# Bucket bits by four 32-column products into one bank, and one reading engine for each count bank, in a hash-masked attention and MoE kernel

## The chip, the cores and the metric

The kernel runs on one core of a Trainium2 chip. The metric is device time in microseconds, from the start of the program to its end; runs are compared by their median.

A core has a matrix engine (TensorE, PE in the rows), whose weight loads (PEld) overlap its products, and three engines for elementwise work: VectorE (DVE), ScalarE (ACT) and GpSimd (POOL). Each takes its own instructions in order. Transfers are issued on a fifth queue, SyncE's (SP). Products land in PSUM, in banks of 128 partitions x 512 floats.

## The reference

Attention with a bucket mask, then a gated MLP (SiLU), then an MLP (ELU). The part that the change touches is the mask: a query sees only keys of its own bucket, and a bucket is the six signs of the head's vector times `proj`.

```python
q_bits = (np.einsum('bhsd,dk->bhsk', q, proj) > 0).astype(np.int64)
k_bits = (np.einsum('bhsd,dk->bhsk', k, proj) > 0).astype(np.int64)
q_bucket = np.sum(q_bits * powers, axis=-1)
k_bucket = np.sum(k_bits * powers, axis=-1)
mask = q_bucket[:, :, :, None] == k_bucket[:, :, None, :]
scores = scale * np.matmul(q, k.transpose(0, 1, 3, 2))
scores = np.where(mask, scores, -1000000000.0)
scores = scores - np.max(scores, axis=-1, keepdims=True)
attn = np.exp(scores)
attn = attn / (np.sum(attn, axis=-1, keepdims=True) + 1e-09)
return np.matmul(attn, v).astype(np.float32)
# then, on x of (1536, 512), with x = norm(attention):
#   y   = (silu(xn @ w_gate) * (xn @ w_val)) @ w_out      d_ff 1536
#   out = elu(y @ w_in) @ w_out2                          d_ff 2048
```

There are 2 batches of 8 heads, 768 positions and 64 channels a head, all in fp32; the MLP weights arrive as 64-bit floats.

## The kernel before

**Pairs.** The 16 heads are taken in eight pairs (index `j`; the head in the pair is `a`). A pair's inputs come in six transfers of 384 KB: for each head `qk` (query over key, 64 channels each, 128 partitions), `kk` (key twice) and `qq` (query twice).

**Operands.** A head's scores are one product over 256 rows in two steps of 128 partitions, in the fast fp32r format. The operands are `tq` (query side) and `tk` (key side), each of two planes of 128 x 768. Three quarters of them hold the rounded vector and its rounding rest; the last 64 rows of plane 1 hold the bucket code: `tk` a +-1 per bucket, `tq` a value of 2^60 in the row of its own bucket, so that a score outside the bucket falls far below the others. GpSimd makes the query side in `operand_q`: `upper` casts the upper 64 partitions (L405), `lower` multiplies the lower 64 by the scale (L412), a transfer copies the result (`dup`, L416) and `lo` subtracts (L420). ScalarE and GpSimd make the key side in `operand_k` (L375, L382).

**Bits and counts.** `prep_bits` multiplies a pair's `qk` by `proj` in plain fp32, for each half of the positions (`hf`, 384 columns) once: two products, one a head, summed into one bank `ps_b` (L442). The columns of `pj` are laid so that the query and key bits of both heads stand in 24 partitions. VectorE compares that bank with zero into `bitt` (L447, 24 x 384, two a pair); a row of ones in `bitt` carries a constant. `prep_count` then multiplies `bitt` by a table `wsel` for the query side (`i` = 0) and the key side (`i` = 1) and each half: four banks `ps_c` a pair (L461), 64 partitions of a bank to each head. Each bank is read twice (`hot`), once a head, into `tq` or `tk`: by VectorE (L472) and by ScalarE (L470), as `HOT = ('DVE', 'ACT', 'ACT', 'DVE')` says, so that each bank has one reader on either engine.

**The rest of attention.** Per 128 queries: four score products into a double bank `ps_s` (L517), a maximum (VectorE `nm`, L524), an exponential (ScalarE `p`, L534); per 256 queries three groups of transposes into a bank `ps_p` (L562), split into rounded part and rest `pt` (ScalarE L570, VectorE L574; or GpSimd L583, L586), and products with the values in `ps_v` (L609). There are four single banks, shared by `ps_b`, `ps_c`, `ps_p`, `ps_v` and the norm's banks, and two double banks. While pairs run, the engines also turn the first MLP weights into two fp32r tensors each (L851 to L900).

**The MLPs** follow on TensorE as three-pass fp32r products (`ps_h` L949, `ps_y` L1034, `ps_o` L1089), with the other engines splitting the hidden values and preparing further weights beside them.

**The order.** Every step is a task in a list with its engine, a planned cost and what it needs. The numbers in `ORDER` are the tasks in the order in which they are issued, over all engines; that order is fixed in the file, and the planned costs do not act at run time. Each engine runs its own instructions in that order and waits for what they need. At the start TensorE runs products without use (`ps_w`, L1150) until inputs are there.

Of the kernel before, what the change touches and what calls it, by code (L numbers as in the profile page):

```python
# [225 lines left out]
def kernel(  # L226
# [53 lines left out]
    def f(ap):  # L280
        return ap.bitcast(F32)

    ident = const.tile([128, 128], F32, name="ident")
    pj = const.tile([128, 2, 128], F32, name="pj")
    wsel = const.tile([128, 2, 128], F32R, name="wsel")
    bitt = [const.tile([128, S], F32R, name=f"bitt{i}") for i in range(2)]
    ones = const.tile([128, 128], F32, name="ones")
# [986 lines left out]
```

## Time and profile before

| | us |
|---|---|
| median of 3 runs (838.7 to 840.76) | 839.86 |
| the profiled execution | 840.58 |
| its span in the trace | 838.8 |
| TensorE busy, of the span | 816.9 (97%) |
| VectorE busy | 602.1 (72%) |
| ScalarE busy | 416.8 (50%) |
| GpSimd busy | 328.1 (39%) |

The profiled execution took 1.78 us more than its span and 0.72 us more than the median. The shares of the whole span mix two stages: the pairs, up to about 265 us, and the MLPs behind them. A matmul's busy time is modelled, and a product is counted for longer than the distance to the next one. So the distance between products, read from the chain of waits, says what a product costs, and the stretches say which engine has slack.

### The profile page before, as it was taken

Reading aid. Unit: us, or ns where it says so; the run is one execution under the profiler, and the core shown is the slowest. Engines: PE = TensorE matmul, PEld = TensorE weight load, DVE = VectorE, ACT = ScalarE, POOL = GpSimd, SP = SyncE. Lnnn points to the kernel's source line nnn. Section 1 sums busy time; section 2 is a strip of 40 time slices with the busy share of each in tenths; the row PEclk is TensorE's granted clock in tenths of the full one; section 3 lists DMA queues with packets and bytes.
Section 4 is the critical chain, followed back from the end, with each engine's and each line's share of the span. In section 5 each row is a group of like instructions: output and inputs, shape, how many; then the busy total and the mean of one; then the engine's idle time right before and its main releaser. Section 6 shows DMA issues by size and latency. Waiting matters only on the chain.

```text
span 838.8 us, 11843 instructions
## 1 busy us (share of the span) xinstructions
PE 816.9 (97%) x4498; PEld 714.1 (85%) x4498; DVE 602.1 (72%) x933; ACT 416.8 (50%) x785; POOL 328.1 (39%) x273
## 2 busy tenths in 40 slices
PE   7999999999899999999999999999999999999998
PEld 6898888888789999898888888888788888888887
DVE  4788899999998683543555564879666768677676
ACT  3898998977888553431222321335454242332321
POOL 7899987898988501100111212021012011110210
PEclk8999999999999999999999999999999999999999
DMA  6525842252103002200302123130322300021004
GB/s 214 165 68 169 275 143 83 67 159 69 39 1 114 1 1 93 71 26 1 131 21 76 51 61 115 39 103 13 111 76 87 102 24 26 26 76 50 1 1 150
DMA packets 28473, 64.99 MB, mean 77 GB/s; under 512 B 2816, under 2 KB 3584, under 8 KB 28416
## 3 DMA queue, kind: packets, MB, share of 16 engines
q1 hardware_dynamic: 28416, 64.24, 23.8%
q8 instruction: 35, 0.57, 0.3%
q14 instruction: 22, 0.18, 0.1%
HBM read 57.94 MB, written 3.15 MB: 73 GB/s over the span
## 4 chain that ended last, share of the span: by engine, by line
PE 77%; DVE 11%; ACT 7%; issue 2%; POOL 1%; DMA 1%; SPq 0%; ACTq 0%; DVEq 0%; POOLq 0%
PE ps_h L949 36%; PE ps_o L1089 15%; PE ps_y L1034 10%; PE ps_v L609 5%; PE ps_s L517 5%; PE ps_p L562 4%; DVE pt L574 2%; DVE nm L524 2%; ACT p L534 2%; ACT pt L570 2%; PE ps_b L442 1%; DVE wf L867 1%; DMA kk<-in_heads_dram 1%; DVE wf L874 1%; DVE ya L1046 1%
## 5 line engine op out<-in xcount | busy, mean ns | idle before, releaser
L900 POOL TENSOR_TENSOR wlo<-wf,whi 128x768 fp32r<-128x768 f32 (+1 forms) x54 | 88.4, 1650 | 448.3 <-ACT whi L896 387.4
L949 PE MATMUL ps_h<-xn,whi 128*128 128x512 f32 (+2 forms) x768 | 190.2, 336 | 0.0
L949 PEld LDWEIGHTS ps_h<-xn,whi 128*128 128x128 f32 x768 | 133.8, 189 | 11.9
L995 ACT CAST h<-hf 128x512 fp32r<-128x512 f32 (+1 forms) x87 | 52.1, 606 | 179.3 <-DVE hf L980 60.5
L949 PE MATMUL ps_h<-xn,wlo 128*128 128x512 f32 (+2 forms) x384 | 128.9, 336 | 0.0
L1089 PE MATMUL ps_o<-whi,h 128*128 128x512 f32 (+1 forms) x388 | 118.6, 387 | 0.4 <-DVE ya L1046 0.4
L949 PE MATMUL ps_h<-y,whi 128*128 128x512 f32 x384 | 118.2, 389 | 0.0
L517 PE MATMUL ps_s<-tk,tq 128*128 128x384 f32 x384 | 90.8, 359 | 8.7 <-ACT p L534 6.4
L609 PE MATMUL ps_v<-pt,vv 128*128 128x256 f32 x576 | 94.4, 294 | 2.1 <-DVE pt L574 1.0
L524 DVE TENSOR_REDUCE nm<-ps_s 128x1 f32<-128x768 f32 x96 | 90.8, 947 | 7.4 <-PE ps_s L517 6.5
L999 DVE TENSOR_TENSOR h<-hf,h 128x512 fp32r<-128x512 f32 (+1 forms) x87 | 64.5, 756 | 41.5 <-ACT h L995 41.3
L1034 PE MATMUL ps_y<-h,whi 128*128 128x512 f32 (+1 forms) x312 | 91.6, 374 | 0.8 <-DVE ya L1046 0.7
L534 ACT ACTIVATE p<-ps_s,nm 128x768 f32<-128x768 f32 x96 | 87.1, 908 | 8.5 <-DVE nm L524 7.7
L574 DVE TENSOR_TENSOR pt<-ps_p,pt 128x512 fp32r<-128x512 f32 x120 | 80.0, 682 | 12.9 <-ACT pt L570 12.0
L562 PE MATMUL ps_p<-ident,p 128*128 128x128 f32 x576 | 84.6, 278 | 2.9 <-DVE pt L574 2.2
L1089 PEld LDWEIGHTS ps_o<-whi,h 128*128 128x128 f32 x388 | 72.6, 188 | 15.5 <-DVE ya L1046 0.8
L974 ACT ACTIVATE sg<-ps_h 128x512 f32<-128x512 f32 (+1 forms) x87 | 49.4, 580 | 72.3 <-PE ps_h L949 53.3
L949 PEld LDWEIGHTS ps_h<-y,whi 128*128 128x128 f32 x384 | 72.1, 188 | 14.9
L609 PEld LDWEIGHTS ps_v<-pt,vv 128*128 128x128 f32 x576 | 78.8, 189 | 5.4 <-DVE pt L574 2.2
L562 PEld LDWEIGHTS ps_p<-ident,p 128*128 128x128 f32 x576 | 67.6, 142 | 12.0 <-DVE pt L574 5.1
L949 PEld LDWEIGHTS ps_h<-xn,wlo 128*128 128x128 f32 x384 | 72.6, 189 | 5.7
L517 PEld LDWEIGHTS ps_s<-tk,tq 128*128 128x128 f32 x384 | 64.3, 191 | 14.9 <-ACT p L534 10.8
(91 smaller groups left out, 1366.4 us busy)
## 6 DMA issues: line engine op xcount, KB each, us to landing
wraw<-in_moe_w_out_dram SPq DMA_DIRECT2D x12, 768.0 KB, 4.7
qq<-in_heads_dram SPq DMA_DIRECT2D x16, 384.0 KB, 4.2
qk<-in_heads_dram SPq DMA_DIRECT2D x16, 384.0 KB, 4.7
kk<-in_heads_dram SPq DMA_DIRECT2D x16, 384.0 KB, 4.0
wraw<-in_moe_w_in_dram SPq DMA_DIRECT2D x8, 768.0 KB, 5.6
wraw<-in_moe_w_out_dram SPq DMA_DIRECT2D x10, 512.0 KB, 3.6
vn<-in_v_dram SPq DMA_DIRECT2D x8, 384.0 KB, 3.5
wraw<-in_moe_w_gate_dram SPq DMA_DIRECT2D x4, 768.0 KB, 5.4
```

The lines of the kernel that those rows point to most:

```text
L517: nc.tensor.matmul(st[B_][:, hf, 0:HS], lhsT=tq[:, x, c * 128:(c + 1) * 128], rhs=tk[:, x, hf * HS:(hf + 1) * HS], start=(x == 0), stop=(x ...
L524: nc.vector.tensor_reduce(out=st["nm", u, cc], in_=st[B_][:, :, 0:HS], axis=AX.XY, op=ALU.max, negate=True,)
L534: nc.scalar.activation(out=halves(st["p", u][:, cc]), in_=st.pop(B_)[:, :, 0:HS], func=AF.Exp, bias=st["nm", u, cc], scale=1.0, accum_out= ...
L562: nc.tensor.transpose(out=st[B_][:, o:o + 128], in_=p[:, cc, (2 * n + kt) * 128:(2 * n + kt + 1) * 128], identity=ident,)
L574: nc.vector.tensor_tensor(out=pt[:, 1], in0=st.pop(B_), in1=f(pt[:, 0]), op=ALU.subtract)
L609: nc.tensor.matmul(st[B_][:, 0:256], lhsT=st["vv", j][:, a, 2 * n + kt, :], rhs=pt[:, x, kt * 256:(kt + 1) * 256], start=(n == seq[0] and ...
L900: nc.gpsimd.tensor_tensor(out=l, in0=s["w"], in1=f(h), op=ALU.subtract)
L949: nc.tensor.matmul(ps[:, o:o + ln], lhsT=w[wp][:, kk, ft * 128:(ft + 1) * 128], rhs=t[xp][:, s:s + ln], start=(kk == 0 and n == 0), stop=( ...
L995: nc.scalar.copy(out=st["h", g, blk, ft][:, 0, 0:bw], in_=s["hf"])
L999: nc.vector.tensor_tensor(out=h[:, 1, 0:bw], in0=s["hf"], in1=f(h[:, 0, 0:bw]), op=ALU.subtract)
L1034: nc.tensor.matmul(s["ps"][:, 0:bw], lhsT=wo[wp][:, ft, m * 128:(m + 1) * 128], rhs=h[:, xp, 0:bw], start=(ft == 0 and i == 0), stop=(ft = ...
L1089: nc.tensor.matmul(s["ps"], lhsT=h[:, xp, t * 128:(t + 1) * 128], rhs=wo[wp][:, ft, ds], start=(ft == 0 and i == 0), stop=(ft == n - 1 and ...
```

## The change

It does five things.

1. **Bits.** `pj` becomes 128 x 32: the six columns of `proj` for the query channels, six for the key channels, the rest zero. A pair's four products (two halves, two heads) each go to their own group of 32 partitions of one bank. `bitt` becomes 128 x 384. One comparison a pair, with a threshold per partition (`floor`: 0, and -1 in the first row of each group, which makes the row of ones).
2. **Counts.** `wsel` has a half more as an index, with zeros in the rows of the other half; the four count products a pair stay, each over all of `bitt`.
3. **Readers.** `HOT = ('DVE', 'ACT')`: VectorE reads both heads of a query bank, ScalarE both heads of a key bank. The number of reads is the same on either engine.
4. **Query operand.** `upper` and `lower` become one GpSimd instruction over all 128 partitions with a scale per partition and a second multiplication by 1.0.
5. **Order and planned costs.** A new `ORDER` for the whole program, and some planned costs.

```diff
+BITS = 1.8
-HOT = ('DVE', 'ACT', 'ACT', 'DVE')
+HOT = ('DVE', 'ACT')
-QENG = ["Pool"] * 16
 ORDER = [
-    9, 0, 6, 5, 1, 7, 56, 50, 53, 2, 8, 48, 51, 57, 59, 49, 28, 10, 12, 13, 14, 15, 16, 17, 54, 55, 11, 60, 61, 68,
...
-    pj = const.tile([128, 2, 128], F32, name="pj")
-    wsel = const.tile([128, 2, 128], F32R, name="wsel")
-    bitt = [const.tile([128, S], F32R, name=f"bitt{i}") for i in range(2)]
+    pj = const.tile([128, 32], F32, name="pj")
+    wsel = const.tile([128, 2, 2, 128], F32R, name="wsel")
+    bitt = [const.tile([128, S // 2], F32R, name=f"bitt{i}") for i in range(2)]
+    floor = const.tile([128, 1], F32, name="floor")
...
         def both():
-            nc.scalar.activation(
-                out=operand(j, a, 0)[:, 0, cs], in_=st["x", j, a, 2][:, cs], func=AF.Copy, scale=share[:, 1:2]
-            )
+            nc.gpsimd.tensor_scalar(
+                out=operand(j, a, 0)[:, 0, cs], in0=st["x", j, a, 2][:, cs], scalar1=share[:, 1:2], scalar2=1.0,
+                op0=ALU.mult, op1=ALU.mult,
+            )
...
-            plan.add("Pool", 0.12 + n * 0.00092, upper, [X_], los, prio)
...
-                plan.add("Pool", 0.12 + n * 0.00092, lower, [X_], his, prio)
+        plan.add("Pool", 0.17 + n * 0.00105, both, [X_, "share"], his + los, prio)
...
         def pe():
             st[B_] = bank("ps_b")
-            for a in range(2):
-                nc.tensor.matmul(
-                    st[B_][:, 0:HS], lhsT=pj[:, a], rhs=st["x", j, a, 0][:, cs], start=(a == 0), stop=(a == 1)
-                )
+            for hf in range(2):
+                for a in range(2):
+                    g = 64 * hf + 32 * a
+                    nc.tensor.matmul(
+                        st[B_][g:g + 32, 0:HS], lhsT=pj, rhs=st["x", j, a, 0][:, hf * HS:(hf + 1) * HS],
+                        start=True, stop=True,
+                    )
 
         def bits():
             nc.vector.tensor_scalar(
-                out=bitt[j % 2][0:M, cs], in0=st.pop(B_)[0:M, 0:HS], scalar1=0.0, scalar2=None,
-                op0=ALU.is_gt,
-            )
+                out=bitt[j % 2], in0=st.pop(B_)[:, 0:HS], scalar1=floor[:, 0:1], scalar2=None, op0=ALU.is_gt,
+            )
...
-                st[B_][:, 0:HS], lhsT=wsel[:, i, :], rhs=bitt[j % 2][:, cs], start=True, stop=True
+                st[B_][:, 0:HS], lhsT=wsel[:, hf, i, :], rhs=bitt[j % 2], start=True, stop=True
...
-            eng = HOT[2 * i + a]
+            eng = HOT[i]
...
-    dma(lambda: nc.sync.dma_start(out=pj, in_=proj), 128 * 1024, [], ["pj"], -29.93)
+    dma(lambda: nc.sync.dma_start(out=pj, in_=proj), 128 * 128, [], ["pj"], -29.93)
```

The transfers at the start stand in another order on SyncE's queue. Before (names as above; `wtmp` is the table, `vn` the values):

```order
L322 DMA qq<-in_heads_dram 128x768
L322 DMA qk<-in_heads_dram 128x768
L1144 DMA pj<-in_proj_dram 128x256
L322 DMA qk<-in_heads_dram 128x768
L322 DMA kk<-in_heads_dram 128x768
L1137 DMA wtmp<-in_table_dram 128x256
L322 DMA kk<-in_heads_dram 128x768
L322 DMA qq<-in_heads_dram 128x768
```

And now:

```order
L321 DMA qk<-in_heads_dram 128x768
L1126 DMA pj<-in_proj_dram 128x32
L321 DMA qk<-in_heads_dram 128x768
L321 DMA qq<-in_heads_dram 128x768
L321 DMA kk<-in_heads_dram 128x768
L1119 DMA wtmp<-in_table_dram 128x256
L332 DMA vn<-in_v_dram 128x768
L405 DMA tq<-tq 64x384
L321 DMA kk<-in_heads_dram 128x768
L321 DMA qq<-in_heads_dram 128x768
```

The second `qk` moved from fourth to third place, behind a smaller `pj`; the first `kk` stayed fifth, and the second moved back from seventh to ninth.

On ScalarE at the start of the program, the reads of pair 0's count banks (L470, now L452) stand about the key operands (L375, now L374). Each `kk` serves one head; the buffer numbers tell the banks apart. Before:

```order
L375 ACTIVATE tk_110<-kk_108,share_86 128x384 x2
L375 ACTIVATE tk_131<-kk_118,share_86 128x384
L470 ACTIVATE tk_110<-ps_c_163 64x384
L470 ACTIVATE tk_110<-ps_c_168 64x384
L470 ACTIVATE tq_134<-ps_c_171 64x384
L470 ACTIVATE tq_134<-ps_c_160 64x384
```

And now:

```order
L374 ACTIVATE tk_137<-kk_135,share_87 128x384 x2
L452 ACTIVATE tk_137<-ps_c_149 64x384
L452 ACTIVATE tk_137<-ps_c_155 64x384
L452 ACTIVATE tk_167<-ps_c_149 64x384
L374 ACTIVATE tk_167<-kk_164,share_87 128x384
```

The first head's reads no longer stand behind the second head's `kk`, and ScalarE no longer reads query banks.

On VectorE in pair 1's preparation, the reads of count banks among the other work. Before:

```order
L472 TENSOR_SCALAR tq_251<-ps_c_299 64x384
L472 TENSOR_SCALAR tk_318<-ps_c_311 64x384
L574 TENSOR_TENSOR pt_325<-ps_p_320,pt_325 128x512
L524 TENSOR_REDUCE nm_345<-ps_s_333 128x1
L627 TENSOR_TENSOR ot_342<-ps_v_267,ot_342 64x256
L524 TENSOR_REDUCE nm_375<-ps_s_358 128x1
L447 TENSOR_SCALAR bitt1_83<-ps_b_352 24x384
```

And now:

```order
L454 TENSOR_SCALAR tq_261<-ps_c_306 64x384
L454 TENSOR_SCALAR tq_309<-ps_c_306 64x384
L555 TENSOR_TENSOR pt_319<-ps_p_314,pt_319 128x512
L505 TENSOR_REDUCE nm_345<-ps_s_328 128x1
L454 TENSOR_SCALAR tq_309<-ps_c_349 64x384
L505 TENSOR_REDUCE nm_358<-ps_s_353 128x1
L454 TENSOR_SCALAR tq_261<-ps_c_349 64x384
```

Both reads of a bank now stand on VectorE: next to each other for bank 306, with a maximum between them for bank 349. A comparison of pair 1 that stood among these rows is gone.

## Rows read from the trace of the kernel before

**Rows 1.** Stretches: busy us (instructions) of each engine, TensorE clock, DMA share, GB/s
```profile
0.00:14.07 14.07, 9.58 (x47) 7.56 (x47) 4.95 (x12) 4.63 (x8) 10.04 (x18) 1.00 0.83 278
14.07:264.50 250.43, 237.27 (x1604) 213.25 (x1605) 226.58 (x342) 212.46 (x432) 224.07 (x193) 0.99 0.34 106
290.00:838.80 548.80, 544.59 (x2683) 468.32 (x2681) 355.09 (x557) 184.30 (x316) 77.38 (x48) 1.00 0.18 59
```

**Rows 2.** The page's chain that ended last: shares of the span
```profile
PE 77%; DVE 11%; ACT 7%; issue 2%; POOL 1%; DMA 1%; SPq 0%; ACTq 0%; DVEq 0%; POOLq 0%
PE ps_h L949 36%; PE ps_o L1089 15%; PE ps_y L1034 10%; PE ps_v L609 5%; PE ps_s L517 5%; PE ps_p L562 4%; DVE pt L574 2%; DVE nm L524 2%; ACT p L534 2%; ACT pt L570 2%; PE ps_b L442 1%; DVE wf L867 1%; DMA kk<-in_heads_dram 1%; DVE wf L874 1%; DVE ya L1046 1%
```

**Rows 3.** Pieces of that chain, up to 275 us: start, us, what
```profile
22.04 1.29 PE ps_b L442 x4
...
132.83 2.13 POOL tq L412
```

**Rows 4.** Instructions on ps_b: ns min/median/max, first and last start us
```profile
L442 PE MATMUL ps_b<-qk,pj x64: 483/486/590, 6.6 to 208.7; 128*128 128x384 f32 x64
L447 DVE TENSOR_SCALAR bitt<-ps_b x16: 534/537/546, 9.1 to 210.8; 24x384 fp32r<-24x384 f32 x16
```

**Rows 5.** Reads of ps_c, the same columns
```profile
L470 ACT ACTIVATE tq<-ps_c x16: 475/488/492, 12.5 to 220.6; 64x384 fp32r<-64x384 f32 x16
L472 DVE TENSOR_SCALAR tq<-ps_c x16: 538/540/551, 13.4 to 215.9; 64x384 fp32r<-64x384 f32 x16
```

**Rows 6.** Who waited for whom: us in total, times, longest us
```profile
PEld ps_s L517 <- ACT p L534: 10.8, 16, 1.7
...
ACT tq L470 <- DVE tq L472: 5.9, 6, 1.3
...
PEld ps_p L562 <- DVE pt L574: 5.1, 10, 0.9
...
DVE tq L472 <- ACT tq L470: 4.1, 4, 2.5
ACT tk L470 <- DVE tk L472: 3.7, 4, 1.5
...
DVE tk L472 <- ACT tk L470: 2.8, 3, 1.7
```

**Rows 7.** GpSimd's groups by form: busy us, mean ns
```profile
L412 POOL TENSOR_SCALAR tq<-qq 64x768 fp32r<-64x768 f32 x14 | 29.9, 2133 | 1.2
...
L405 POOL CAST tq<-qq 64x768 fp32r<-64x768 f32 x14 | 11.9, 848 | 0.4
...
L741 POOL TENSOR_SCALAR z<-z 128x384 f32<-128x384 f32 x2 | 1.0, 514 | 0.2
```

**Rows 8.** Timeline of the start: start us, us, what [idle before, releaser]
```profile
8.16 2.20 PE L442 MATMUL ps_b<-qk,pj 128*128 128x384 f32 x6 [0.77 <-DMA qk<-in_heads_dram]
...
9.18 1.12 ACT L375 ACTIVATE tk<-kk,share 128x384 fp32r<-128x384 f32 x2 [7.19 <-DMA kk<-in_heads_dram]
...
9.59 0.34 DVE L1155 CAST wsel<-wtmp 128x256 fp32r<-128x256 f32 x1
...
9.87 2.94 POOL L382 TENSOR_TENSOR tk<-kk,tk 64x384 fp32r<-64x384 f32 x3
...
11.13 0.61 ACT L375 ACTIVATE tk<-kk,share 128x384 fp32r<-128x384 f32 x1 [0.83 <-DMA kk<-in_heads_dram]
...
13.42 0.55 DVE L472 TENSOR_SCALAR tq<-ps_c 64x384 fp32r<-64x384 f32 x1 [2.47 <-ACT tq L470]
...
14.07 1.55 PE L517 MATMUL ps_s<-tk,tq 128*128 128x384 f32 x6 [2.10 <-DVE tq L472]
```

**Rows 9.** Stretches of the start, columns as in rows 1
```profile
17.00:19.00 2.00, 2.00 (x7) 2.00 (x8) 1.22 (x3) 1.14 (x3) 1.85 (x3) 0.50 0.49 172
...
23.00:25.00 2.00, 2.00 (x16) 1.87 (x15) 1.83 (x4) 1.54 (x5) 1.94 (x3) 1.00 0.04 10
```

**Rows 10.** TensorE's waits from 268 us on, columns as in rows 6
```profile
PE ps_y L1034 <- DVE ya L1046: 0.7, 2, 0.5
```

More of the change, by code (lines that the diff above doesn't have):

```diff
@@ L398, in both @@
         def both():
-            nc.scalar.activation(
-                out=operand(j, a, 0)[:, 0, cs], in_=st["x", j, a, 2][:, cs], func=AF.Copy, scale=share[:, 1:2]
-            )
-        def upper():
-            out, in_ = operand(j, a, 0)[up, 0, cs], st["x", j, a, 2][up, cs]
-            nc.gpsimd.tensor_copy(out=out, in_=in_)
-        def lower():
-            out, in_ = operand(j, a, 0)[dn, 0, cs], st["x", j, a, 2][dn, cs]
-            if how == "mixed":
-                nc.scalar.activation(out=out, in_=in_, func=AF.Copy, scale=QSCALE)
-            else:
-                nc.gpsimd.tensor_scalar(out=out, in0=in_, scalar1=QSCALE, scalar2=None, op0=ALU.mult)
+            nc.gpsimd.tensor_scalar(
+                out=operand(j, a, 0)[:, 0, cs], in0=st["x", j, a, 2][:, cs], scalar1=share[:, 1:2], scalar2=1.0,
+                op0=ALU.mult, op1=ALU.mult,
+            )
         def dup():
@@ L422, in operand_q, with prep_bits @@
         his, los, dups = ([okey(j, a, 0, (p, h)) for h in cols] for p in ("hi", "lo", "dup"))
-        if how == "ACT":
-            plan.add("ACT", act(n) + 0.15, both, [X_, "share"], his + los, prio)
-        else:
-            plan.add("Pool", 0.12 + n * 0.00092, upper, [X_], los, prio)
-            if how == "mixed":
-                plan.add("ACT", act(n) + 0.05, lower, [X_], his, prio)
-            else:
-                plan.add("Pool", 0.12 + n * 0.00092, lower, [X_], his, prio)
+        plan.add("Pool", 0.17 + n * 0.00105, both, [X_, "share"], his + los, prio)
         dma(dup, 64 * n * 4, his, dups, prio)
         plan.add("Pool", pool(n), lo, [X_], los, prio)
-    def prep_bits(j, hf, prio):
-        cs = slice(hf * HS, (hf + 1) * HS)
-        B_ = ("bank", "b", j, hf)
-        M = 4 * NB
+    def prep_bits(j, prio):
+        B_ = ("bank", "b", j)
         def pe():
             st[B_] = bank("ps_b")
-            for a in range(2):
-                nc.tensor.matmul(
-                    st[B_][:, 0:HS], lhsT=pj[:, a], rhs=st["x", j, a, 0][:, cs], start=(a == 0), stop=(a == 1)
-                )
+            for hf in range(2):
[5 more added lines that the diff above has]
+                    )
         def bits():
             nc.vector.tensor_scalar(
-                out=bitt[j % 2][0:M, cs], in0=st.pop(B_)[0:M, 0:HS], scalar1=0.0, scalar2=None,
-                op0=ALU.is_gt,
-            )
-        plan.add("PE", 8 * mm(HS) - 0.09, pe, [*(("h3", "x", j, a, 0) for a in range(2)), "pj"], [B_], prio)
-        plan.add("DVE", dve(HS), bits, [B_, "bitt"], [(("bits", j), hf)], prio)
+                out=bitt[j % 2], in0=st.pop(B_)[:, 0:HS], scalar1=floor[:, 0:1], scalar2=None, op0=ALU.is_gt,
+            )
+        plan.add("PE", BITS, pe, [*(("h3", "x", j, a, 0) for a in range(2)), "pj"], [B_], prio)
+        plan.add("DVE", dve(HS), bits, [B_, "floor"], [("bits", j)], prio)
     def prep_count(j, i, hf, prio):
@@ L486, in prep @@
         p = prio
-        for hf in range(2):
-            prep_bits(j, hf, p)
-            p += step
+        prep_bits(j, p)
+        p += 2 * step
         for i in range(2):
@@ L1122, in setup_bits @@
     def setup_bits():
-        for t in bitt:
-            nc.vector.memset(f(t), 0.0)
-            nc.vector.memset(f(t[32:33]), 1.0)
+        nc.vector.memset(floor, 0.0)
+        for g in range(4):
+            nc.vector.memset(floor[32 * g:32 * g + 1], -1.0)
+        nc.vector.memset(f(wsel), 0.0)
     def setup2():
@@ L1152, with spread_table @@
     for n in range(WARM):
-        plan.add("PE", 0.218, lambda n=n: warm(n), ["ident"], [("bank", "warm")], 1e6)
+        plan.add("PE", 0.25, lambda n=n: warm(n), ["ident"], [("bank", "warm")], 1e6)
     dma(ld_table, 128 * 1024, [], [("h3", "wtmp")], -29.92)
-    plan.add("DVE", 0.35, lambda: nc.vector.tensor_copy(out=wsel, in_=st["wtmp"]), [("h3", "wtmp")], ["wsel"], -28)
+    def spread_table():
+        for hf in range(2):
+            rows = slice(64 * hf, 64 * hf + 64)
+            nc.vector.tensor_copy(out=wsel[rows, hf], in_=st["wtmp"][rows])
+    plan.add("DVE", 0.55, spread_table, [("h3", "wtmp"), "wzero"], ["wsel"], -28)
     load_v(0, -27)
@@ L1236, in _laid_out @@
     v = v.reshape(B * H // 2, 2, S // 128, 128, D).transpose(0, 3, 1, 2, 4)
-    wide = np.zeros((2, D, 2, 128), proj.dtype)
-    table = np.zeros((128, 2, 128), np.float32)
+    wide = np.zeros((2, D, 32), proj.dtype)
+    table = np.zeros((4, 32, 2, 128), np.float32)
     for i in range(2):
-        for a in range(2):
-            o = (2 * i + a) * nb
-            wide[i, :, a, o:o + nb] = proj
+        o = 1 + i * nb
+        wide[i, :, o:o + nb] = proj
+        for g in range(4):
+            a = g % 2
             for n in range(2 ** nb):
                 for b in range(nb):
-                    table[o + b, i, 64 * a + n] = 1.0 if n >> b & 1 else -1.0
-                table[32, i, 64 * a + n] = 1.0 - bin(n).count("1") - i
-    return dict(rest, heads=heads, v=v, proj=wide.reshape(2 * D, 2, 128), table=table)
+                    table[g, o + b, i, 64 * a + n] = 1.0 if n >> b & 1 else -1.0
+                table[g, 0, i, 64 * a + n] = 1.0 - bin(n).count("1") - i
+    return dict(rest, heads=heads, v=v, proj=wide.reshape(2 * D, 32), table=table.reshape(128, 2, 128))
 def kernel(**inputs):
```

24 lines of the change are left out of this document (12 added, 12 removed), and 277 rows, old and new, of the table ORDER.

## Prediction

> **What bounds the kernel now.** I read the chain that ended last first, over the whole span [rows 2]: 77% of it is TensorE, and the three MLP products alone are 61%. Then I cut the span where the stages change [rows 1]. From 290 us to the end TensorE is busy 544.6 of 548.8 us; the longest wait there after 268 us is 0.7 us in total [rows 10], and the rest of the idle time is the last addition and store. The work of that stage is the same before and after, so it moves with the moment at which the pairs are done and gives nothing itself.
>
> The pairs are another matter. From 14.07 us to 264.50, where the first MLP product starts (250.4 us), TensorE is busy 237.3, VectorE 226.6, GpSimd 224.1, ScalarE 212.5 [rows 1]. No engine is full, all four are at 85 to 95%, and they wait for each other in turn: the largest waits of TensorE there are on the exponential (10.8 us) and on the subtraction that frees a bank (5.1 us) [rows 6]. So a microsecond taken from one engine is worth between nothing and a microsecond, and I look for work that leaves both of the fullest engines. Before 14.07 us TensorE does nothing for the scores: that is the start, whose length is a chain of loads and small steps [rows 8].
>
> **1. The products for the bits.** There are 32 products in the program before and after. The trace has 64 records of them [rows 4], two a product. On the chain two products take 1.29 us [rows 3], so a record's distance to the next is 1.29/4 = 0.32 us, and a pair costs 2.58 us. No trace of before shows products in groups of 32 partitions. The bounds: all four side by side, two records long, 0.64 us; none side by side, 2.58 us, and the switch to narrow groups and back lets the pipeline empty each time. For emptying I take what a record lasts beyond its distance, 0.486 - 0.32 = 0.16 us [rows 4], twice: 2.91 us. Between them I reason from the order of the instructions. TensorE takes them in turn; the two records of one product write the same group and must follow each other; the second of one and the first of the next are in different groups. So five distances, 1.61 us, and one tail of 0.16: 1.8 us. I take that, since it needs only what the records show. It saves 0.8 us a pair, 5.6 us in the seven pairs behind the start; the ends are +2.3 and -13.6 us.
>
> The Trainium skill has a rule for more and one for less. Its page TensorEngine Tiling (Array Packing), section Theoretical Speedup, gives up to four times for an output of 32 columns; the page TensorE: Matmul & The Clock Gate, Part 3, gives 2.38 times measured with three column tiles. By 2.38 (an estimate from that page) a pair would cost 1.1 us and the seven would save 10.5 us. The first page's Key Properties say that a change of tiling mode drains the engine, which speaks against the change. No row here shows either.
>
> **2. The comparisons.** Sixteen of 0.537 us become eight of the same length, since the columns stay 384 and only the partitions grow [rows 4]. Seven of the saved ones lie behind the start: VectorE does 3.8 us less. A dearer one, by the threshold read per partition, would show in a longer row; I take the old duration.
>
> **3. One reader a bank.** The number of reads and their durations (0.54 on VectorE, 0.49 on ScalarE [rows 5]) stay. What goes is the turn: the second reader waits for the first. VectorE waited 4.1 + 2.8 us for ScalarE's reads and ScalarE 5.9 + 3.7 us for VectorE's [rows 6]. Of VectorE's 6.9 us, 2.5 belong to the start [rows 8]; 4.4 remain. What takes their place is a read behind other work of the same engine, which costs the engine nothing but holds the bank (rival below). So VectorE's part of the stretch shrinks by 3.8 + 4.4 = 8.2 us if the rest of its work keeps its pace. ScalarE gets 9.6 us more slack, which I count at nothing: it has 38 us of it [rows 1].
>
> **4. The query operand on GpSimd.** A cast of 0.848 and a multiplication of 2.133 us become one instruction on 128 partitions [rows 7]. The nearest row for the new one is the multiplication with two operations on 128 x 384, 0.514 us, twice that for 768 columns: 1.03 us. The far ends are 0.85 and 2.13. GpSimd loses 14 x (2.98 - 1.03) = 27 us, at least 12. It was late for others in one place that I find on the chain, where the old multiplication stands with 2.13 us [rows 3]. So I take 0, with 3 us for the lower end. The transfer of the result and the subtraction behind it also start earlier, which helps the same step.
>
> **5. The start.** Scores run without a break from 14.07 us, when VectorE's first `tq` is done; that read began at 13.42 after 2.47 us of waiting for ScalarE's read of the same bank [rows 8]. ScalarE was late because it stood at the second `kk`, whose wait ended at 11.13. In the new order that key step stands behind the first head's two key reads, and no query read waits for ScalarE. New times, from the rows: the second `qk` comes one load earlier (1.95 us for 512 KB between the two `kk`, 9.18 to 11.13, so 1.46 a load, and 0.43 for the smaller `pj`): 8.16 - 1.9 = 6.3. Bits until 8, comparison until 8.7. The table's cast is at 9.59 as before at the latest, since its load is sixth again. Counts at 9.9, VectorE's read until 10.8. ScalarE's two key operands end at 10.3 as now, its two key reads at 11.4. GpSimd's two key rests start when the first key operand is there (one of two in 1.12 us, so 9.75) and take 0.98 us each (three in 2.94): 11.7. So the scores start at about 12.2 instead of 14.07: -1.8 us; the ends are 0 (the table or a load late) and -2.2.
>
> The clock hangs on the start. The granted clock is 0.50 (1.2 GHz) from 17 to 21 us while TensorE is busy without a break, and 1.00 (2.4 GHz) from 23 on [rows 9]; before the fall it had waited 2.1 us for a read [rows 8]. A start with fewer waits may be spared that: some 5 us of work at half speed, so at most -2.5. A start with another gap may have it for 2 us longer. I take 0.
>
> **6. The new order as such** changes what waits where in all of the 250 us. But for the edits above it holds the same instructions, and the first MLP product stands behind the same 1601 products of TensorE. I count it at 0 and give it 4 us either way.
>
> **The sum.** Behind the start TensorE alone would give -5.6 and VectorE alone -8.2. The two depend on each other, so I take the middle, -7. With the start, -8.8. The profiled execution took 840.58 us, so 831.8; the median of the runs lies 0.7 lower, so **831.1 us**. With the order's 4 us and the ends of the start (1.8 and -0.4) this case reaches from 826.5 to 837.
>
> **Rivals.**
>
> *All four products side by side.* Then a pair costs 0.64 + 0.16 = 0.8 us and TensorE saves 12.4 us behind the start, and VectorE follows, because its waits on scores shrink. 840.6 - 1.8 - 12.4 = 826.4, on the runs' scale 825.7; with the clock spared 823. For it: the groups share no partition. Against: two records of one product stand in one group, and VectorE at 226.6 - 3.8 of some 238 us would be at 94%. Chance 0.13. It is what the Trainium skill's page TensorEngine Tiling (Array Packing), section Theoretical Speedup, promises for 32 columns.
>
> *The bits do not get shorter.* The groups run one after the other and both switches cost a tail: 2.91 us a pair, +2.3 us behind the start. TensorE then sets the pace, and VectorE's 8.2 us become waiting: 840.6 - 1.8 + 2.3 = 841.1, on the runs' scale 840.4. That is the change not doing what it says. For it: nothing in the trace shows two products at once. Chance 0.07. The Trainium skill's rule that a change of mode drains the engine (the same page, Key Properties) would work towards it.
>
> *The gain goes to steps that are not touched.* VectorE has more room, but the maximum, the exponential and the two halves of `pt` are on the chain with 2% of the span each [rows 2], and they are as long as before. Then only the start and a share of the bits come through: 840.6 - 1.8 - 1 = 837.8, or 837.1 on the runs' scale, up to 839.5 if the start gives half. Chance 0.11.
>
> *Slower: the single banks run short.* Four banks serve bits, counts, transposes and values. A count bank is free when both reads are done, and both now stand on one engine; in 8 of the 28 banks behind the start other work stands between them, as in the rows shown of VectorE's order. TensorE waited 5.1 us already for a transposed bank to be freed [rows 6]. If each of the 28 banks holds TensorE up by one read (0.54 us), 15.1 us come on top: 846.2. It makes the kernel slower by over 0.3% from 11.3/28 = 0.40 us a bank. Against it: the old turn held banks as well, 16.5 us over 17 waits [rows 6], and two banks a pair for bits become one. Chance 0.12.
>
> **How the numbers follow.** A measurement of this kernel can tell about 0.3% (2.5 us) from no change: faster is below 837.3, slower above 842.4. Forecast 0.57, side by side 0.13, untouched steps 0.11 (0.05 of it below 837.3), no shorter 0.07, banks 0.12. Faster 0.57 + 0.13 + 0.05 = 0.75, same 0.06 + 0.07 = 0.13, slower 0.12. The range leaves out most of the bank case and the far end of the side-by-side case, and holds the rest: 822.5 to 841.5.
>
> **What would show it.** Products on `ps_b`: a pair at 1.8 us on TensorE (0.8: side by side; over 2.6: no shorter). Eight comparisons at 0.54. No wait of ScalarE for VectorE's reads or the reverse. GpSimd's new instruction at 1.0 us, and some 25 us less of it. First unbroken scores near 12.2 us. First `ps_h` near 256 instead of 264.5, and as many microseconds from there to the end as now, 574.3; if that grows, the new order has put a wait into the MLPs, and the forecast is wrong in the part that I counted at nothing.

## The result, and the profile after

The changed kernel takes 824.5 us (median of 4 runs, 824.36 to 824.97) against 840.11 us before (4 runs): a ratio of 0.982, 95% interval 0.980 to 0.983, so 15.6 us or 1.8% faster. The forecast was 831.1 us, in a range of 822.5 to 841.5: the sign was right, and 6.6 us of gain were missing. The rival "all four products side by side" had 825.7.

The stretches of the kernel after, cut where its stages change (columns as in [rows 1]: busy us and instructions of PE, PEld, DVE, ACT, POOL; clock; DMA share; GB/s), and the first MLP product:

```profile
0.00:12.52 12.52, 8.20 (x45) 6.74 (x46) 3.84 (x13) 3.60 (x6) 4.65 (x11) 0.98 0.69 220
12.52:248.60 236.08, 223.45 (x1607) 202.12 (x1607) 225.98 (x335) 214.48 (x435) 195.50 (x183) 0.99 0.39 120
274.00:822.60 548.60, 544.67 (x2684) 468.50 (x2682) 355.58 (x555) 186.11 (x317) 79.26 (x48) 1.00 0.18 59
```
```profile
L930 PE MATMUL ps_h<-xn,whi x768: 277/334/521, 248.6 to 545.7; 128*128 128x512 f32 x72, 128*128 128x256 f32 x72, 128*128 128x384 f32 x48
```

From 248.6 us to the end of the span are 574.0 us, before 574.3 [rows 1]: the MLPs gave nothing and took nothing. The span is 16.2 us shorter. With the cut at the scores that the prediction names, the start gave 14.07 - 12.52 = 1.55 of that, and the pairs 250.43 - 236.08 = 14.35. In the pairs TensorE's busy time fell by 237.27 - 223.45 = 13.8 us, and its idle time hardly changed (13.2 to 12.6). VectorE's busy time did not change (226.6 to 226.0), but its idle time fell from 23.9 to 10.1: it is now busy for 96% of the stretch.

The instructions of the changed steps, as in [rows 4, 5] (ns min/median/max, first and last start us):

```profile
L424 PE MATMUL ps_b<-qk,pj x64: 483/486/510, 6.0 to 194.3; 128*32 128x384 f32 x64
L430 DVE TENSOR_SCALAR bitt<-ps_b,floor x8: 598/617/618, 6.9 to 197.2; 128x384 fp32r<-128x384 f32 x8
...
L452 ACT ACTIVATE tk<-ps_c x32: 469/487/494, 10.6 to 204.6; 64x384 fp32r<-64x384 f32 x32
L454 DVE TENSOR_SCALAR tq<-ps_c x32: 540/554/561, 11.2 to 208.6; 64x384 fp32r<-64x384 f32 x32
```

TensorE's timeline at one pair's bits (start us, us, what):

```profile
71.22 0.85 PE L424 MATMUL ps_b<-qk,pj 128*32 128x384 f32 x8
72.00 0.96 PE L498 MATMUL ps_s<-tk,tq 128*128 128x384 f32 x4
```

The same eight records in two narrower windows:

```profile
71.22 0.53 PE L424 MATMUL ps_b<-qk,pj 128*32 128x384 f32 x4
```
```profile
71.56 0.51 PE L424 MATMUL ps_b<-qk,pj 128*32 128x384 f32 x4
```

Eight records, each still 0.49 us long, start in two rounds of four, 0.34 us apart, and the next product starts 0.78 us after the first of them. So the four products run side by side, and a pair's bits cost 0.8 us where they cost 2.58.

The longest waits of the pairs, 12 to 245 us (us in total, times, longest):

```profile
ACT p L515 <- DVE nm L505: 10.3, 14, 1.8
...
PEld ps_s L498 <- ACT p L515: 6.6, 10, 2.4
PEld ps_p L543 <- DVE pt L555: 5.6, 11, 1.7
...
DVE pt L555 <- ACT pt L551: 3.8, 14, 0.5
```

No wait between ScalarE's and VectorE's reads of a count bank is left, and TensorE waits 6.6 us for exponentials where it waited 10.8 [rows 6]. VectorE's wait for ScalarE's half of the probabilities, 7.7 us before, is 3.8. What ScalarE waits for most is VectorE's maximum, 10.3 us now and 7.7 before. The chain of waits says the same: VectorE's share of it rose from 11% [rows 2] to 14%, and `ps_b` is gone from it:

```profile
PE 78%; DVE 14%; ACT 5%; issue 2%; DMA 1%; SPq 0%; DVEq 0%; ACTq 0%
```

### The profile page after: what moved, and what is told of

Its sections match the earlier page's. It is cut to its first block, busy times and chain, and to the rows that moved or that the text cites. A ratio compares the mean times of both kernels' runs of the same rounds, so it can differ in the third digit from the quotient of the medians.

```text
span 822.6 us, 11863 instructions
## 1 busy us (share of the span) xinstructions
PE 801.7 (97%) x4498; PEld 702.1 (85%) x4498; DVE 601.8 (73%) x928; ACT 419.5 (51%) x785; POOL 295.9 (36%) x255
## 4 chain that ended last, share of the span: by engine, by line
PE 78%; DVE 14%; ACT 5%; issue 2%; DMA 1%; SPq 0%; DVEq 0%; ACTq 0%
PE ps_h L930 40%; PE ps_o L1070 16%; PE ps_y L1015 12%; DVE nm L505 4%; DVE pt L555 4%; PE ps_v L590 3%; PE ps_p L543 3%; PE ps_s L498 3%; ACT p L515 2%; ACT pt L551 1%; DMA wtmp<-in_table_dram 1%; DVE ot L608 1%; DVE wf L835 1%; DVE tq L454 1%; ACT tk L374 1%
## 5 line engine op out<-in xcount | busy, mean ns | idle before, releaser
L881 POOL TENSOR_TENSOR wlo<-wf,whi 128x768 fp32r<-128x768 f32 (+1 forms) x54 | 90.7, 1687 | 455.2 <-ACT whi L877 383.8
L930 PE MATMUL ps_h<-xn,wlo 128*128 128x256 f32 (+2 forms) x384 | 128.9, 336 | 0.0
L515 ACT ACTIVATE p<-ps_s,nm 128x768 f32<-128x768 f32 x96 | 87.0, 906 | 11.3 <-DVE nm L505 10.5
L498 PE MATMUL ps_s<-tk,tq 128*128 128x384 f32 x384 | 88.7, 354 | 3.8 <-ACT p L515 3.5
L980 DVE TENSOR_TENSOR h<-hf,h 128x512 fp32r<-128x512 f32 (+1 forms) x87 | 66.4, 776 | 31.3 <-ACT h L976 30.8
L543 PEld LDWEIGHTS ps_p<-ident,p 128*128 128x128 f32 x576 | 65.9, 141 | 12.8 <-DVE pt L555 5.6
L1027 DVE TENSOR_TENSOR ya<-ps_y,ya 128x512 f32<-128x512 f32 x48 | 32.8, 688 | 59.5 <-PE ps_y L1015 59.5
```

What stands on the lines that cost most here:

```text
L498: nc.tensor.matmul(st[B_][:, hf, 0:HS], lhsT=tq[:, x, c * 128:(c + 1) * 128], rhs=tk[:, x, hf * HS:(hf + 1) * HS], start=(x == 0), stop=(x ...
L515: nc.scalar.activation(out=halves(st["p", u][:, cc]), in_=st.pop(B_)[:, :, 0:HS], func=AF.Exp, bias=st["nm", u, cc], scale=1.0, accum_out= ...
L543: nc.tensor.transpose(out=st[B_][:, o:o + 128], in_=p[:, cc, (2 * n + kt) * 128:(2 * n + kt + 1) * 128], identity=ident,)
L881: nc.gpsimd.tensor_tensor(out=l, in0=s["w"], in1=f(h), op=ALU.subtract)
L930: nc.tensor.matmul(ps[:, o:o + ln], lhsT=w[wp][:, kk, ft * 128:(ft + 1) * 128], rhs=t[xp][:, s:s + ln], start=(kk == 0 and n == 0), stop=( ...
L980: nc.vector.tensor_tensor(out=h[:, 1, 0:bw], in0=s["hf"], in1=f(h[:, 0, 0:bw]), op=ALU.subtract)
```

## The experiments

The first expectations weigh four theories. A: the edits pay, and the order is only another one. B: the new order pays. C: of the edits, TensorE's shorter bits pay. D: VectorE sets the pace, and of the edits the end of the turn at the count banks is worth most. Prices below are differences of medians to the changed kernel's 824.5; ratios are to the kernel before, measured again beside each group of runs (839.6 to 840.0), with 95% intervals.

One table for all of them, from each profile's stretch between 12.5 us and the first `ps_h`. The profile is of one execution, which can lie off the median (by 1.6 us at wide bits, by 2.8 at old steps in the new order), and the first scores come between 10.96 and 13.01 us, so a microsecond in these columns decides nothing.

| kernel | median us | stretch | TensorE busy | idle | VectorE idle | clock |
|---|---|---|---|---|---|---|
| before | 840.1 | 252.0 | 237.3 | 14.7 | 24.8 | 0.99 |
| after | 824.5 | 236.1 | 223.5 | 12.6 | 10.1 | 0.99 |
| edits, old order | 842.0 | 253.8 | 232.3 | 21.5 | 29.8 | 0.97 |
| old steps, new order | 856.8 | 271.3 | 241.2 | 30.1 | 43.3 | 0.97 |
| wide bits | 829.0 | 242.4 | 233.3 | 9.1 | 16.1 | 0.99 |
| readers in turn | 840.2 | 253.5 | 230.1 | 23.4 | 32.8 | 0.97 |
| operand in two parts | 842.7 | 254.4 | 229.6 | 24.8 | 26.4 | 0.97 |
| comparison twice | 827.0 | 241.5 | 226.5 | 15.0 | 12.9 | 0.97 |
| operand twice | 828.8 | 240.9 | 226.0 | 14.9 | 15.3 | 0.99 |
| more products at the start | 824.9 | 236.4 | 224.0 | 12.4 | 10.5 | 0.99 |
| more probabilities on GpSimd | 830.3 | 240.3 | 224.5 | 15.8 | 16.7 | 0.99 |
| maximum on GpSimd | 826.4 | 238.2 | 224.3 | 13.9 | 15.4 | 0.99 |
| old order, no new readers | 839.2 | 251.6 | 230.6 | 21.0 | 26.4 | 0.98 |
| old order, bits only | 846.4 | 258.8 | 234.4 | 24.4 | 32.8 | 0.96 |

**Edits or order.** Two kernels take them apart. In the first every task of the changed kernel stands where its counterpart stood before (a task made from two at the first of them; the setting of the per-partition scale goes to the front). In the second the tasks of the kernel before stand in the new order.

```diff
 # first: the changed kernel
-ORDER = [...]   # new
+ORDER = [...]   # old, in the changed kernel's numbers
 # second: the kernel before
-ORDER = [...]   # old
+ORDER = [...]   # new, in the numbers of the kernel before
```

> All edits of the change, with the steps in the order of the kernel before (a step that two old steps became stands where the first of them stood). Theory A, the edits themselves pay: 825 to 830 us, first MLP product at 249 to 254 us. Theory B, the new order pays: 836 to 841 us. If both are needed, 830 to 836.

Measured: 841.98 us, ratio 1.002 (1.000 to 1.003).

> The kernel before with the steps in the new order (the two old steps for one new one stand next to each other in its place). Theory A: 838 to 846 us, no gain, since the old work does not fit the places of the new. Theory B: 825 to 832 us.

Measured: 856.79 us, ratio 1.021 (1.018 to 1.023).

Neither A nor B holds. The edits alone give nothing, the order alone costs 17 us, and both together give 15.6. With the edits in the old order TensorE's busy time does fall (237.3 to 232.3), but its idle time rises by 6.8.

**The bits.** The changed kernel with full-width products: four copies of `pj`, each with zeros outside its own 32 columns, summed into the same bank.

```diff
-                        st[B_][g:g + 32, 0:HS], lhsT=pj, rhs=..., start=True, stop=True,
+                        st[B_][:, 0:HS], lhsT=pjw[:, g // 32], rhs=..., start=(g == 0), stop=(g == 96),
```

> The changed kernel with the four bit products of a pair 128 columns wide, summed into the one bank, so that they take 2.6 us of TensorE a pair again instead of 0.8; all else as changed. Theory C, TensorE's shorter bits are the gain: 1.8 us in each of seven pairs come back, 12.6 us, so 837 us. Theory D, VectorE sets the pace of the pairs and TensorE has slack: 825 to 829 us.

Measured: 828.98 us, ratio 0.988 (0.985 to 0.990): 4.5 us. TensorE has 9.8 us more to do in the stretch, and its idle time falls by 3.5: with VectorE nearly full, part of what the narrow products save was idle time anyway. C named far too much: without the narrow products 11.1 of the 15.6 us stay.

**The readers.** The changed kernel with each count bank read by both engines in turn, everything else as after.

```diff
-HOT = ('DVE', 'ACT')
+HOT = ('DVE', 'ACT', 'ACT', 'DVE')
...
-            eng = HOT[i]
+            eng = HOT[2 * i + a]
```

> The changed kernel with the old readers: each count bank is read once by VectorE and once by ScalarE, in the places of the new order. Theory D with the turn as its largest part: VectorE waits for ScalarE again, 4 to 10 us come back, 829 to 835 us. If the turn is worth nothing: 824 to 826 us.

Measured: 840.19 us, ratio 1.001 (0.999 to 1.002): 15.7 us, the whole gain. The turn is back in the waits of this kernel (12.5 to 245 us), three times as long as the 4.4 us that the kernel before had behind the start [rows 6, 8]:

```profile
DVE tq L451 <- ACT tq L449: 7.8, 5, 3.3
...
DVE tk L451 <- ACT tk L449: 5.9, 5, 2.5
```

That is 13.7 us on the engine that has least to spare. One of these waits on VectorE's timeline, and what TensorE and its clock do around it (busy us, granted clock, DMA share, GB/s in each two microseconds):

```profile
215.24 0.43 DVE L605 TENSOR_TENSOR ot<-ps_v,ot 64x256 f32<-64x256 f32 x1
218.13 0.56 DVE L451 TENSOR_SCALAR tk<-ps_c 64x384 fp32r<-64x384 f32 x1 [2.47 <-ACT tk L449]
```
```profile
214.00:216.00 2.00, 1.32 (x9) 1.00 0.00 0
216.00:218.00 2.00, 1.59 (x9) 1.00 0.03 8
218.00:220.00 2.00, 1.24 (x7) 1.00 0.00 0
220.00:222.00 2.00, 0.72 (x5) 0.57 0.00 0
222.00:224.00 2.00, 2.00 (x11) 0.50 0.00 0
224.00:226.00 2.00, 2.00 (x10) 0.50 0.00 0
226.00:228.00 2.00, 2.00 (x13) 0.72 0.00 0
228.00:230.00 2.00, 2.00 (x16) 1.00 0.00 0
```

ScalarE had exponentials and halves of probabilities ahead of its read; VectorE stood for 2.47 us, TensorE thinned out behind it, and then its clock was granted at 0.50 (1.2 GHz) for some six microseconds: 10 to 11 products in 2 us instead of 16. Three such places in this trace (from 96, 124 and 220 us) go with 6.6 us more busy time for the same products; 10.8 us are idle time. From 17 to 260 us the trace of the changed kernel has no such place. The clock is not what makes the loss: four executions of this kernel with a mean granted clock of 0.997 to 0.998, as high as in the changed kernel's, took 838.6 to 840.2 us.

**GpSimd's operand.** The changed kernel with the query operand in two parts as before.

```diff
-            nc.gpsimd.tensor_scalar(out=operand(j, a, 0)[:, 0, cs], in0=st["x", j, a, 2][:, cs],
-                scalar1=share[:, 1:2], scalar2=1.0, op0=ALU.mult, op1=ALU.mult)
+            o, x = operand(j, a, 0)[:, 0, cs], st["x", j, a, 2][:, cs]
+            nc.gpsimd.tensor_copy(out=o[up], in_=x[up])
+            nc.gpsimd.tensor_scalar(out=o[dn], in0=x[dn], scalar1=QSCALE, scalar2=None, op0=ALU.mult)
```

> The changed kernel with the query operand in two GpSimd instructions as before (a cast and a one-operation multiplication, 2.98 us a head instead of 0.93). GpSimd gets 14 x 2.05 = 29 us more behind the start, and would be busy 224 of 236 us. If GpSimd's room is no part of the gain, 824 to 827 us; if it is, since the operands then come late, 830 to 838 us.

Measured: 842.69 us, ratio 1.004 (1.002 to 1.006): 18 us. GpSimd's timeline shows why this counts in the new order. First the changed kernel, then this one:

```profile
21.65 0.92 POOL L398 TENSOR_SCALAR tq<-qq,share 128x768 fp32r<-128x768 f32 x1 [0.66 <-DMA qq<-in_heads_dram]
22.50 0.62 POOL L564 CAST pt<-pf 128x512 fp32r<-128x512 f32 x1
23.09 0.93 POOL L398 TENSOR_SCALAR tq<-qq,share 128x768 fp32r<-128x768 f32 x1
23.96 1.30 POOL L567 TENSOR_TENSOR pt<-pf,pt 128x512 fp32r<-128x512 f32 x1
```
```profile
25.48 2.13 POOL L397 TENSOR_SCALAR tq<-qq 64x768 fp32r<-64x768 f32 x1
27.67 0.61 POOL L560 CAST pt<-pf 128x512 fp32r<-128x512 f32 x1
28.22 0.82 POOL L396 CAST tq<-qq 64x768 fp32r<-64x768 f32 x1
29.12 2.13 POOL L397 TENSOR_SCALAR tq<-qq 64x768 fp32r<-64x768 f32 x1
31.33 1.26 POOL L563 TENSOR_TENSOR pt<-pf,pt 128x512 fp32r<-128x512 f32 x1
```

The new order has an operand between the rounded part and the rest of a group of probabilities `pt`, and TensorE's value products wait for both. With 0.93 us it fits; with 2.95 it does not, as TensorE's timeline of this kernel shows:

```profile
28.33 0.50 PE L586 MATMUL ps_v<-pt,vv 128*128 128x256 f32 x2 [1.89 <-POOL pt L560]
32.65 0.79 PE L586 MATMUL ps_v<-pt,vv 128*128 128x256 f32 x2 [3.81 <-POOL pt L563]
```

In the whole stretch TensorE waits 11.3 us for GpSimd, where the changed kernel has no such wait; its idle time grew by 12.2. The 11.3 us are these two rows and the first wait above:

```profile
PE ps_v L586 <- POOL pt L563: 5.8, 3, 3.8
PE ps_s L494 <- POOL tk L378: 3.6, 3, 2.6
```

The clock is granted at 0.50 behind such waits in this kernel too (from 31, 62 and 191 us). The kernel with old steps in the new order has the same row of steps on GpSimd at 29.7 us, and TensorE is idle from 32 to 34 us there. So the new order rests on the short operand, and GpSimd's idle time in the sum of the stretch says nothing on that. The 18 us are the price of both parts one behind the other, where the new order has the operand; in the kernel before they stood apart, and two parts laid out apart in the new order were not tried.

**Smaller doses.** If those two are places that cannot take a delay, more work in small pieces should cost less. VectorE's comparison was made twice (4.3 us more, in 7 pieces), and GpSimd's operand twice (13 us more, in 14).

```diff
+                for n in range(2):   # the comparison into bitt; in the other kernel the operand
```

> The changed kernel with each pair's comparison done twice: 0.62 us more of VectorE a pair, 4.3 us in the seven pairs behind the start. Theory D, VectorE sets the pace: 3 to 5 us slower, 827.5 to 829.5 us. If TensorE does, 824.5 to 826 us.

Measured: 827.01 us, ratio 0.984 (0.981 to 0.987). No execution lies there: two took 825.0 us, with a mean granted clock of 0.999, and two 829.0 and 829.3, with 0.994 and 0.991. So the 4.3 us of work cost 0.5 us where the clock held and 4.5 where it fell (in the trace, of 829.3 us, it is at half from 12 to 20 us and near it from 96 to 100), and the median of 2.5 us decides for neither theory.

> The changed kernel, with GpSimd's new query operand instruction issued twice (the second writes the same values again). GpSimd has 14 x 0.93 = 13 us more to do behind the start, about half of what the operand in two parts added (28.7 us, which cost 18 us). Theory 'price': what the operand costs is paid per microsecond of GpSimd, 18/28.7 = 0.63: 8 us slower, 832-834. Theory 'room': GpSimd has 40 us of idle time in the stretch, and what cost was only the long delay of a single operand (2.98 us); 13 us fit in: 824-827.

Measured: 828.76 us, ratio 0.986 (0.984 to 0.989): 4.3 us of 13, between the two theories (its four executions lie between 826.4 and 829.8). TensorE waits for GpSimd's probabilities once in its stretch, for 2.6 us. The operand in two parts added 2.2 times as much work and cost 4 times as much, which fits a price that grows with the length of the single delay; neither a price per microsecond nor the room in the sum gives it.

**The parts in the old order.** The changed kernel's edits in the old order again, but without the new readers; and, of the edits, with the bits and the comparison alone.

```diff
 # edits in the old order, and
-HOT = ('DVE', 'ACT')
+HOT = ('DVE', 'ACT', 'ACT', 'DVE')
 # in the second also the operand in two parts, as above
```

> The old order with the narrow bits, the single comparison and GpSimd's operand of the changed kernel, but each count bank read by both engines in turn as before. Theory 'fit' (each order is good for the work it was laid out with, and a part gains little in an order made for other work): 837-841, like the kernel before and like all edits in the old order (842). Theory 'own price' (the parts have the prices measured in the new order, bits 4.5, comparison 2.5, operand up to 18, and in the old order the one reader a bank took it all away): 815-828.

Measured: 839.24 us, ratio 0.999 (0.999 to 1.000).

> The old order with the narrow bits and the single comparison alone; operand in two parts and readers in turn as before. This is the part that the prediction priced with 5.6 + 3.8 us (half way between engines: 4.7). Theory 'own price' (4.5 for the bits and 2.5 for the comparison, as in the new order): 833. Theory 'fit': the shortened steps only lengthen the waits for other engines: 838-841.

Measured: 846.35 us, ratio 1.007 (1.005 to 1.009): 6.5 us slower than the kernel before.

In the first of the two, "fit" holds and "own price" falls. The second settles less than it was meant to, because it is not the kernel before with narrow bits alone. In the kernel before, the cast and the multiplication of a query operand stood apart in the order; here both stand at the place of the first, which brings the multiplication of 2.13 us forward. GpSimd's rows in the third pair, before and in the second kernel:

```profile
52.26 1.83 POOL L382 TENSOR_TENSOR tk<-kk,tk 64x768 fp32r<-64x768 f32 x1
54.17 1.81 POOL L420 TENSOR_TENSOR tq<-qq,tq 64x768 fp32r<-64x768 f32 x1
56.05 2.13 POOL L412 TENSOR_SCALAR tq<-qq 64x768 fp32r<-64x768 f32 x1
```
```profile
52.35 2.13 POOL L397 TENSOR_SCALAR tq<-qq 64x768 fp32r<-64x768 f32 x1
54.56 1.82 POOL L405 TENSOR_TENSOR tq<-qq,tq 64x768 fp32r<-64x768 f32 x1
56.45 1.80 POOL L378 TENSOR_TENSOR tk<-kk,tk 64x768 fp32r<-64x768 f32 x1
```

The key rest now comes behind the multiplications, 4.2 us later, and TensorE's scores wait for it:

```profile
54.79 0.62 PE L494 MATMUL ps_s<-tk,tq 128*128 128x384 f32 x2 [0.15 <-ACT p L511]
58.31 0.62 PE L494 MATMUL ps_s<-tk,tq 128*128 128x384 f32 x2 [2.91 <-POOL tk L378]
```

Behind this gap the clock falls here too (0.50 from 60 to 62 us). With GpSimd's short operand the loss goes away (846.4 to 839.2), but these 7.1 us are the price of an operand that was long and moved as well, not of the old one; what the narrow bits alone do in the old order stays open. With one reader a bank 2.7 us come on top again (842.0, executions from 839.3 to 843.9, against 838.4 to 840.5 without). So in the old order the new readers cost some 2 to 3 us; in the new one they give 15.7.

**Three tries at a better kernel**, none of which was one. The first gives TensorE more to do without use at the start:

```diff
-        nc.tensor.matmul(st["warm"][:, 0:128], lhsT=ident, rhs=ident, start=True, stop=True)
+        for _ in range(3 if n > 8 else 1):
+            nc.tensor.matmul(st["warm"][:, 0:128], lhsT=ident, rhs=ident, start=True, stop=True)
```

> The changed kernel with three products without use in place of one in the second block at the start (from 6.8 us), so that TensorE is busy until the counts. If the granted clock of 0.50 from 11.5 to 15.4 us follows the waits before it and costs time, the clock stays at 1.00 there and the time falls by 1 to 2 us, 822.5 to 823.5 us. If VectorE or the loads hold the start, 824 to 825 us; if the added products delay the counts, 825 to 826 us.

Measured: 824.91 us, ratio 0.983 (0.981 to 0.984): no change, though the mean granted clock from 12.5 to 30 us was 1.00 and not 0.92. (In the changed kernel's trace it is at 0.50 from 12 us on, not from 11.5.) The first scores come at 12.58 us, where they came at 12.52, which leaves inputs and counts as the bound of the start.

The second splits more groups of probabilities on GpSimd, in 3 and not 2 of a pair's six blocks of 256 queries, in pairs 3 to 6:

```diff
-BYPOOL = (..., [2, 4], [2, 4], [2, 4], [2, 4], [0])
+BYPOOL = (..., [0, 2, 4], [0, 2, 4], [0, 2, 4], [0, 2, 4], [0])
```

> The changed kernel with one more of the six row blocks of a pair, in pairs 3 to 6, whose first group of transposes is split by GpSimd instead of ScalarE and VectorE: VectorE loses 4 x 0.68 = 2.7 us, GpSimd gains 4 x 2 = 8 us. Theory D: 1.5 to 3 us faster, 821.5 to 823 us. If GpSimd comes too late for the products with the values: 824.5 to 828 us.

Measured: 830.33 us, ratio 0.989 (0.987 to 0.991): 5.8 us slower, though VectorE does less (223.6 us in the stretch, where it was 226.0). The third moves a step on the weights from VectorE to GpSimd:

```diff
+                if g == 0:
+                    nc.gpsimd.tensor_scalar(out=s["w"], in0=s["w"], scalar1=LEAST, scalar2=1.0, op0=ALU.max, op1=ALU.mult)
+                    return
```

> The changed kernel with one of VectorE's four steps on the first group of weights (the maximum of `wf`, 128 x 768, six behind the start at 1.31 us each) moved to GpSimd. VectorE is busy 226 of the 236 us of pairs, GpSimd 195. Theory 'VectorE sets the pace': it loses 7.8 us of work and half to all of it comes through: 817-821. Theory 'fit': the step stands where GpSimd was not meant to have one, and delays its weights of probabilities or operands; like the probabilities moved to it (+5.8): 825-831.

Measured: 826.44 us, ratio 0.984 (0.982 to 0.985): 1.9 us slower. The step takes 2.78 us there, and VectorE's three other steps on the same tile got longer on average (1.40 us each in place of 1.18): its busy time fell by 3.2 us (226.0 to 222.8) and not by 7.8.

```profile
L833 POOL TENSOR_SCALAR wf<-wf x6: 2773/2778/2789, 82.8 to 206.1; 128x768 f32<-128x768 f32 x6
```

## Why the prediction was right, and where it was not

- **What bounds the kernel**: right. All of the gain lies in the pairs and the start, and the MLPs moved with them.
- **Step 1, bits, 1.8 us a pair**: wrong by a factor of two. I took the records in the order of the products, so that the two of one product are neighbours and must follow each other: five distances. The trace has two rounds of four: 0.78 us is two distances (0.64) and a tail (0.14), the side-by-side rival's price to 0.02 us. TensorE's saving behind the start is 7 x 1.80 = 12.6 us, not 5.6, and it is the larger part of the 13.8 us by which its busy time fell; the clock, half for some 3 us of the start instead of some 6, goes with most of the rest. But only 4.5 us of the kernel's time hang on it. The Trainium skill's page TensorEngine Tiling (Array Packing), section Theoretical Speedup, says up to four times for 32 columns; the trace agrees, with 2.58/0.78 = 3.3. The Trainium skill has a change of mode drain the engine (the same page, Key Properties); that would fit into the 0.14 us, but no row here tells it apart.
- **Step 2, comparisons at 0.54 us**: 0.617, so 14 x 0.537 - 7 x 0.617 = 3.2 us and not 3.8. Both the threshold per partition and the partitions (128, not 24) are new in it; which of them makes it longer, no run shows.
- **Step 3, turn waits**: right that they end and on which engine they weigh. Their price was read from the old order, 4.4 us; put back into the new one they are 13.7 us, and the kernel loses 15.7.
- **Step 4, GpSimd's operand**: 0.93 us was right (1.03 forecast), and "0, with 3 us for the lower end" was the worst number of the forecast: back in two parts, the operand costs 18.2 us. I looked for the place where the operand is late in the old order. The new order puts it between probabilities, which no row of before could price, but the order of the instructions on GpSimd had it to read.
- **Step 5, the start**: 12.52 us where 12.2 was forecast, -1.55 and not -1.8. Counts waited for the table's cast, two instructions of 1.79 us together where I had one of 0.34. "Without a break from 14.07" misread the trace: two score products had run at 11.46 us, and those from 14.07 stop again at 15.6 for 1.1 us. And over all the kernels here the first scores come between 10.96 and 13.01 us, so 1.55 us between two executions says little.
- **Step 6, the order at 0 within 4 us**: the step that failed in its form. The order is worth -17.5 us with the edits and +17 without them. The sum added the parts as if each had its own price; their prices hang on where the order has put the work that waits for them.
- **The sum**: half way between TensorE's -5.6 and VectorE's -8.2. With the right bits that would be the middle of -12.6 and -7.6, -10.1, and the pairs gave -14.35, more than either. VectorE's idle time fell by 13.8 us, and TensorE's stayed as it was: with the new order, readers and operand together, VectorE kept up with all that TensorE saved. That a sum of parts came within 6.6 us is partly luck: taken back one at a time, bits, readers and operand cost 4.5, 15.7 and 18.2 us, 38 in all, of a gain of 15.6. Two of its small figures do not come out: the near end of the forecast's case is 831.1 - 4.4 = 826.7, not 826.5, and untouched steps with half of the start end at 839.0, not 839.5. Neither moves the range.
- **Rivals**: "side by side" came closest (825.7), and it was right on the products. That its time is off by only 1.2 us is luck: it has all of TensorE's 12.4 us come through, and with wide products the kernel loses 4.5. "Single banks run short" fell: in the changed kernel the waits of TensorE that end with the read of a count bank come to 1.0 us in all (0.7 before transposes, 0.3 before counts), 0.04 us a bank where 0.40 would decide.

What stays open: what the narrow bits alone give in the old order; whether another order would get something out of them, or all of it out of the old readers or the old operand. No order was laid out for these kernels, and the two at hand differ in every pair.

## What to carry to other kernels

Where a hand-made order fits several full engines together, an edit has no price of its own: one reader a bank was worth 15.7 us in the new order here, and cost 2 to 3 us in the old one. For each step that gets shorter or longer, read from the new order what stands directly behind it on its engine and who waits for that, and compare the step's length with the slack there, not with the engine's idle time in the stretch. And look at the granted clock behind a stretch of waits on TensorE: in three of the kernels above (readers in turn, operand in two parts, bits only in the old order) it was at half for some microseconds there. When you take a part back to price it, check that nothing else moves with it, as the multiplication did above.

## What the runs showed of the hardware

- Four fp32 products with 32 columns each, in four groups of one bank, cost 0.78 us together, in two rounds of records, where two full-width products of the same length cost 1.29.
- GpSimd's time hangs on the form of the instruction: a multiplication by a constant, one operation, 2.13 us on 64 x 768 (L397 above, L412 in [rows 7]); with a factor per partition and a second operation, 0.93 us on 128 x 768; a maximum and a multiplication, both with constants, 2.78 us on 128 x 768; a multiplication and an addition, both with constants, 0.51 us on 128 x 384 (L741 in [rows 7]).
- VectorE's steps from SBUF to SBUF can stretch beside GpSimd. In the changed kernel the maximum of `wf` (128 x 768) took 0.55 to 0.56 us in all 22 cases in the MLPs, with no GpSimd instruction beside it; in the six in the pairs, all beside GpSimd, it took 0.55 to 2.21. One of these, a step that ran while GpSimd waited, and what GpSimd did then:

```profile
172.71 2.18 DVE L835 TENSOR_SCALAR wf<-wf 128x768 f32<-128x768 f32 x1
...
177.47 0.55 DVE L841 TENSOR_SCALAR wf<-wf 128x768 int32<-128x768 int32 x1
```
```profile
172.08 0.95 POOL L340 CAST vv<-vn 128x384 fp32r<-128x384 f32 x2
173.00 1.46 POOL L675 TENSOR_TENSOR sq<-xT 128x768 f32<-128x768 f32 x1
174.43 1.31 POOL L346 TENSOR_TENSOR vv<-vn,vv 128x384 fp32r<-128x384 f32 x1
177.92 0.61 POOL L564 CAST pt<-pf 128x512 fp32r<-128x512 f32 x1 [2.18 <-ACT pf L560]
```

The second ran while GpSimd waited, in 0.55 us; the first, in 2.18, began beside a cast and ended 0.43 us after GpSimd's `sq`, as if it had run once that was done. The Trainium skill's page SBUF — State Buffer, section SBUF: two separate sides, calls the port pair of the two engines an exclusive lock, held for a whole instruction. These rows fit that but do not prove it. In the pairs VectorE's four weight steps took 27.8 us in 23 instructions, 1.21 us each; the kernel before had 23.5 us in 23, 1.02 each. That is 4.3 us more, which takes up the 3.2 that the comparisons saved, and VectorE's busy time stayed the same.
